# A Fourier-mixing layer in float32 pieces: product 2 of the first transform adds onto a copy of product 1 in an accumulator bank

## The chip, the core and the metric

The kernel runs on one core of a Trainium2 chip. The metric is the time of one execution on the device, in microseconds (us); each number of a run is one execution, and a version's time is the median of its runs. The engines are TensorE (PE in the profile; its weight loads are PEld), VectorE (DVE), ScalarE (ACT), GpSimd (POOL) and SyncE (SP, which here only issues transfers). Matmuls write accumulators into eight banks, each of 128 partitions by 512 float32; ScalarE and VectorE read them from there.

## The reference, cut to what matters

```python
def _A_ref(x, dft_seq_re, dft_seq_im, dft_hid_re, dft_hid_im):
    a = jnp.einsum("bsd,ed->bse", x, dft_hid_re)
    b = jnp.einsum("bsd,ed->bse", x, dft_hid_im)
    y = jnp.einsum("ts,bse->bte", dft_seq_re, a) - jnp.einsum("ts,bse->bte", dft_seq_im, b)
    return y

def _B_ref(x, w1, b1, w2, b2):
    y = _layernorm(x, axis=-1)
    h = _gelu(jnp.einsum("bsd,df->bsf", y, w1) + b1)
    return jnp.einsum("bsf,fd->bsd", h, w2) + b2

x = A_x
xn = _layernorm(x, axis=-1)
s = _A_ref(xn, A_dft_seq_re, A_dft_seq_im, A_dft_hid_re, A_dft_hid_im)
g = _silu(_B_ref(xn, B_w1, B_b1, B_w2, B_b2))
return x + s * g
```

There are 2048 tokens of 512 values, and the hidden layer of `_B_ref` has 1792. The *first transform* is the pair `a`, `b`: along the hidden dimension, with one 512 by 512 matrix for each.

## The kernel before, in words

All matrices are float32. For the matmuls each is split into a high part, rounded by ScalarE (`activation` with Copy into the matmul's input type), and the rest, which VectorE subtracts out; a product is then three matmuls (high by high, high by rest, rest by high).

The stages follow each other on TensorE: the first transform (with the statistics of the layer norm), the first layer of the network (`hy`, `hz`, `hx`), the second layer (`ma`, `mb`), and the second transform along the tokens (`px`, `pz`, `pw`), whose accumulators are multiplied by the gate and written out.

The tokens lie in 16 tiles of 128. Tiles 0 to 5 go through the first transform directly: 12 matmuls into one bank for `a`, 12 for `b` (`dft_mm`, L400; accumulators `pd`), evicted by ScalarE with the token's scale (`dft_out`, L425). Tiles 6 to 15 go in pairs through a scheme that gives the four blocks of a 2 by 2 block product by seven products instead of eight. One pair is done first (tau "u", tiles 6 and 7: accumulators `quy`, `quz`, `qux`), then four pairs (tau 1, chunk c = 0 to 3, tiles 8 + c and 12 + c: `q1y`, `q1z`, `q1x`). Product p has six matmuls per chunk (`q_mm`, L645), and `KEY_Q` says which of three accumulators it uses:

- y: product 1 starts it, then 6, 7 and 4 add to it
- z: product 5 starts it, 3 adds to it
- x: product 2 alone

After products 1, 5, 6 and 4 ScalarE evicts the accumulator, scaled per token, into a tile `e` in the on-chip memory (`q_after`, L631, the instruction at L637). After 2, 3 and 7 VectorE multiplies the accumulator by the scale and adds it to such a tile (L642), which is then a finished block: tile i's part of `a` is product 1 plus product 2. A finished block is appended to a list of stores, which SP issues in order, four behind (`q_out`, L626).

The order of work is written out by hand: each engine executes its instructions in the order of the program text. For the u pair the order of products is 1, 5, 6, 2, 7, 3, 4, with VectorE's work on 2 and 3 put later (`u_after`, L757 to L772). For the four pairs (L777 on) the order is 1, 2, 5, 3, 6, 7, 4, each over the four chunks. Between chunks stand steps that prepare operands of later products: `y_scale` (L542) and `y_sum` (L577) on VectorE, `y_round` on ScalarE (the helper at L77), `y_rest` on VectorE (L81). In product 1 the sum t1, which product 5 needs, is formed by VectorE after chunk 1 and rounded by ScalarE after chunk 2, so ahead of the eviction of chunk 3. In product 2, `post(2, c)` is VectorE's work on chunk c.

Banks come from a pool of eight (`bank`): a new accumulator takes a bank that is free, the one longest free first, and its first writer waits until that bank's last reader is done. The bank of y is taken at product 1, that of x at product 2, that of z at product 5. Tiles `e` come in the same way from the pool `op` of 39 tiles in the on-chip memory. After product 4 the bank pool is closed, and the next layer takes the same eight banks as four accumulators of two banks.

Of the kernel before, what the change touches and what calls it, by code (L numbers as in the profile page):

```python
# [11 lines left out]
AF = mybir.ActivationFunctionType  # L12
ALU = mybir.AluOpType
# [7 lines left out]
def fnet_mixer_kernel(ctx: ExitStack, tc: tile.TileContext, x, xT, ct, wt, w1, w2, b1, b2, out):  # L21
    nc = tc.nc
# [28 lines left out]
    def guest(name):  # L51
        return op.tile([P, 2, W], F32, tag="op", name=name)

    def bank(name):
        return psum.tile([P, W], F32, tag="ps", name=name)
# [366 lines left out]
    def dft_at(i, m):  # L422
        return (b_d if m else a_d)[tok(i) // 2][tok(i) % 2]
# [14 lines left out]
    def store():  # L438
        dst, e = stores.pop(0)
        nc.sync.dma_start(out=dst, in_=e)  # L440
# [165 lines left out]
    qx, q_part = {}, {}  # L606
    Q_TILES = {1: lambda c: (2 * NC + c, 3 * NC + c), "u": lambda c: (NC + CONV + c, NC + CONV + PAIRS + c)}

    def q_scale(tau, t):
        if tau == 1:  # L610
            return qq[:, t - HB:t - HB + 1], nq[:, t - HB:t - HB + 1]
        return rr[:, t:t + 1], nr1[:, t:t + 1]

    def q_at(tau, name, c):
        if tau == "u" and PAIRS == 1:
            return (tau, name in (1, 5)), int(name in (5, 4))
        return (tau, name, c // 2), c % 2

    def q_place(tau, name, c):
        key, at = q_at(tau, name, c)  # L620
        if key not in q_part:
            q_part[key] = guest(f"q{tau}{name}_{c}")
        return q_part[key][:, at, :]


    def q_out(i, m, e):  # L626
        stores.append((dft_at(i, m), e))
        while len(stores) > LAG:
            store()

    def q_after(p, c, tau=1):  # L631
        i, j = Q_TILES[tau](c)
        (f, nf), (g, ng) = q_scale(tau, i), q_scale(tau, j)
        acc = qx[tau, KEY_Q[p], c]
        if p in (1, 5, 6, 4):
            e = q_place(tau, p, c)
            nc.scalar.activation(e, acc, AF.Copy, scale={1: f, 5: ng, 6: g, 4: nf}[p])  # L637
            if p == 4:
                q_out(i, 1, e)
        else:  # L640
            e = q_place(tau, {2: 1, 3: 6, 7: 5}[p], c)
            nc.vector.scalar_tensor_tensor(e, acc, {2: f, 3: g, 7: ng}[p], e, op0=ALU.mult, op1=ALU.add)  # L642
            q_out(*{2: (i, 0), 3: (j, 0), 7: (j, 1)}[p], e)

    def q_mm(p, c, tau=1):  # L645
        key = tau, KEY_Q[p], c
        yh, yl = y_op[RIGHT[p], tau]
        if p in (1, 5, 2):
            qx[key] = bank(f"q{tau}{KEY_Q[p]}{c}")
        cols = slice(c * P, (c + 1) * P)  # L650
        terms = [(a[:, k, cols], w) for k in range(2)
                 for a, w in ((yh, a_op[p][k][0]), (yh, a_op[p][k][1]), (yl, a_op[p][k][0]))]
        for n, (a, w) in enumerate(terms):
            nc.tensor.matmul(qx[key], a, w, start=p in (1, 5, 2) and n == 0,  # L654
                             stop=p in (2, 3, 4) and n == len(terms) - 1, skip_group_check=True)

    def q_product(p, *steps):
        for c in range(NC):
            q_mm(p, c)
            if p in (1, 5, 6, 4):  # L660
                q_after(p, c)
            for do in steps[c:c + 1]:
                for o in do:
                    o()

    def u_product(p):
        for c in range(PAIRS):
            q_mm(p, c, "u")
            if p in (1, 5, 6, 4):
                q_after(p, c, "u")  # L670

    def u_after(p):
        for c in range(PAIRS):
            q_after(p, c, "u")
# [522 lines left out]
    for u, (p, j) in enumerate(m_units):  # L1197
# [3 lines left out]
        if u == 1:  # L1201

            n = NJ - 1
# [5 lines left out]
        n = NJ - 1  # L1209
# [9 lines left out]
        q = m_order.index(p)  # L1219
# [56 lines left out]
    acc, part = {}, {}  # L1276
# [124 lines left out]
```

## Time and profile before

| what | value |
|---|---|
| median of 3 runs | 665.37 us (664.99 to 666.4) |
| the profiled execution, its own time | 665.02 us |
| its span, first to last instruction | 663.2 us |
| its granted TensorE clock | 1.0 |
| matmuls | 2914 |
| first matmul of the u pair, of product 1 on the four pairs, of the next layer | 40.19, 49.73, 87.81 us |

The page of the profile gives the busy time of each engine and its share of the span, then the span in 40 slices (the granted clock in tenths of full speed), and the chain of work that ended last. In the lists, `out<-in` are the program's names for tiles, and L with a number is the line in the code. In an engine's order of time a row gives the start, the length, the engine, the line, the operation, its operands, their size, and in brackets the idle time ahead of it and what ended that. In the grouped list a row ends with the count, the busy time, the mean of one in ns and the idle time ahead of the group.

### The profile page before, as it was taken

What the parts mean: (1) busy time and instruction counts of PE and PEld (TensorE: products, weight loads), DVE (VectorE), ACT (ScalarE), POOL (GpSimd) and SP (SyncE); (2) the same over time, 40 slices, a digit from 0 to 9 for tenths busy, and PEclk for the clock granted to TensorE, in tenths of its full rate; (3) what the DMA queues carried; (4) which work ended last, traced back from release to release, by engine and by line L of the source; (5) the groups of instructions that cost most, each with busy time, mean ns of one, the idle gap of its engine ahead of it and who ended that gap; (6) DMA issues with size and microseconds to landing.
All of it is one profiled execution on the core that took longest, in us unless ns stands there. A gap on an engine that the chain in (4) does not pass through costs nothing.

```text
span 663.2 us, 8219 instructions
## 1 busy us (share of the span) xinstructions
PE 658.2 (99%) x2914; PEld 542.6 (82%) x2914; DVE 543.5 (82%) x584; ACT 361.4 (54%) x420; POOL 50.7 (8%) x84
## 2 busy tenths in 40 slices
PE   9999999999999999999999999999999999999997
PEld 6888888888888888888888888888888888888886
DVE  7899978877776866888979998739877299998986
ACT  6775467544446754555455544456444455646540
POOL 0002000321121100000000000000000001210100
PEclk9999999999999999999999999999999999999999
DMA  9879430987989999798699996416544558996984
GB/s 320 289 266 276 154 140 1 360 314 250 358 302 351 417 411 370 264 385 305 255 386 409 387 326 225 153 51 200 184 156 129 127 137 258 305 257 239 319 251 138
DMA packets 71877, 172.81 MB, mean 261 GB/s; under 512 B 6896, under 2 KB 22812, under 8 KB 71836
## 3 DMA queue, kind: packets, MB, share of 16 engines
q1 hardware_dynamic: 59488, 132.27, 56.7%
q0 software_dynamic: 12032, 39.86, 18.9%
q8 instruction: 23, 0.38, 0.2%
q10 hardware_dynamic: 316, 0.16, 0.1%
q14 instruction: 18, 0.15, 0.1%
HBM read 121.91 MB, written 50.35 MB: 260 GB/s over the span
## 4 chain that ended last, share of the span: by engine, by line
PE 99%; DVE 0%; issue 0%
PE pz L1015 20%; PE px L1015 18%; PE hy L830 11%; PE ma L1015 11%; PE mb L1015 9%; PE hz L830 6%; PE pw L1015 5%; PE pd L406 3%; PE q1y L654 3%; PE hx L830 3%; PE pd L418 2%; PE px L1336 2%; PE pw L1336 2%; PE q1z L654 2%; PE quy L654 1%; PE q1x L654 1%
## 5 line engine op out<-in xcount | busy, mean ns | idle before, releaser
L1121 DVE TENSOR_TENSOR c<-c,c 128x1024 f32<-128x1024 f32 x32 | 39.2, 1224 | 3.4 <-DMA c<-ct 3.4
L81 DVE TENSOR_TENSOR w1l<-w1r,w1h 128x1792 fp32r<-128x1792 f32 x7 | 14.2, 2024 | 20.9 <-ACT w1h L525 20.9
L835 ACT ACTIVATE hc<-hc,b_t 128x1024 f32<-128x1024 f32 (+1 forms) x18 | 17.3, 960 | 25.0 <-DVE hc L875 22.6
L63 DVE TENSOR_TENSOR R_b1l<-c,R_b1h 128x1024 fp32r<-128x1024 f32 x16 | 19.5, 1222 | 13.4 <-ACT R_b1h L62 10.1
L62 ACT ACTIVATE R_s3h<-c 128x1024 fp32r<-128x1024 f32 x16 | 17.0, 1062 | 23.8 <-DVE c L1121 9.8
L1015 PE MATMUL pw<-R_s1h,L 128*128 128x512 f32 x96 | 29.7, 389 | 0.0
L62 ACT ACTIVATE R_b2h<-c 128x1024 fp32r<-128x1024 f32 x16 | 16.9, 1058 | 21.9 <-DVE c L1126 15.5
L63 DVE TENSOR_TENSOR R_s2l<-c,R_s2h 128x1024 fp32r<-128x1024 f32 x16 | 19.6, 1224 | 8.6 <-PE pz L1015 8.6
L62 ACT ACTIVATE R_s2h<-c 128x1024 fp32r<-128x1024 f32 x16 | 17.0, 1060 | 16.8 <-PE px L1015 9.3
L63 DVE TENSOR_TENSOR R_s3l<-c,R_s3h 128x1024 fp32r<-128x1024 f32 x16 | 19.6, 1226 | 3.9 <-PE pz L1015 3.8
L62 ACT ACTIVATE R_s1h<-c 128x1024 fp32r<-128x1024 f32 x16 | 16.4, 1052 | 11.4 <-DVE c L1132 11.4
L1129 POOL DMA_DIRECT2D c<-ct x8 | 7.0, 872 | 200.9 <-DVE c L1126 162.9
L62 ACT ACTIVATE R_b1h<-c 128x1024 fp32r<-128x1024 f32 x16 | 16.6, 1051 | 9.4 <-PE px L1015 4.4
L62 ACT ACTIVATE R_a1h<-c 128x1024 fp32r<-128x1024 f32 x16 | 16.8, 1053 | 8.9 <-PE pz L1015 7.2
L1015 PEld LDWEIGHTS pw<-R_s1h,L 128*128 128x128 f32 x96 | 18.0, 188 | 3.7
L63 DVE TENSOR_TENSOR R_b2l<-c,R_b2h 128x1024 fp32r<-128x1024 f32 x16 | 19.4, 1220 | 1.5 <-PE px L1015 1.5
L63 DVE TENSOR_TENSOR R_a1l<-c,R_a1h 128x1024 fp32r<-128x1024 f32 x16 | 19.6, 1223 | 1.3 <-PE px L1015 1.1
L63 DVE TENSOR_TENSOR R_s4l<-c,R_s4h 128x1024 fp32r<-128x1024 f32 x16 | 19.6, 1226 | 0.7 <-PE px L1015 0.7
L1126 DVE TENSOR_TENSOR c<-c,c 128x1024 f32<-128x1024 f32 x16 | 19.6, 1224 | 0.4
L62 ACT ACTIVATE R_s4h<-c 128x1024 fp32r<-128x1024 f32 x16 | 16.8, 1049 | 5.2 <-PE pz L1015 5.0
L63 DVE TENSOR_TENSOR R_s1l<-c,R_s1h 128x1024 fp32r<-128x1024 f32 x16 | 18.9, 1221 | 0.4 <-ACT R_s1h L62 0.3
L62 ACT ACTIVATE w2h<-w 128x1024 fp32r<-128x1024 f32 (+1 forms) x14 | 13.2, 946 | 10.7 <-DVE w L943 3.9
(1003 smaller groups left out, 2227.3 us busy)
## 6 DMA issues: line engine op xcount, KB each, us to landing
c<-ct SPq DMA_DIRECT2D x68, 512.0 KB, 5.7
m<-h_d SPq DMA_DIRECT2D x48, 512.0 KB, 6.7
h_d<-ht POOLq DMA_DIRECT2D x21, 512.0 KB, 6.8
s_d<-sa SPq DMA_DIRECT2D x32, 256.0 KB, 4.0
la<-s_d SPq DMA_DIRECT2D x32, 256.0 KB, 6.7
h_d<-hc POOLq DMA_DIRECT2D x13, 512.0 KB, 3.8
x<-x SPq DMA_DIRECT2D x16, 256.0 KB, 5.4
sa<-a_d SPq DMA_DIRECT2D x8, 512.0 KB, 6.4
```

Of the source, the lines that this page charges most:

```text
L62: nc.scalar.activation(hi, src, AF.Copy)
L63: nc.vector.tensor_sub(lo, src, hi.bitcast(F32))
L81: nc.vector.tensor_sub(hi_lo[1], src, hi_lo[0].bitcast(F32))
L406: nc.tensor.matmul(acc, xt[i, k][px], weights[m * NK + k][pw], start=n == 0, stop=n == len(terms) - 1)
L418: nc.tensor.matmul(dacc[i, m], xt[i, k][px], weights[m * NK + k][pw], start=seen[i, m] == 0, stop=seen[i, m] == 3 * NK - 1)
L654: nc.tensor.matmul(qx[key], a, w, start=p in (1, 5, 2) and n == 0, stop=p in (2, 3, 4) and n == len(terms) - 1, skip_group_check=True)
L830: nc.tensor.matmul(acc[:, tau, :], w[:, W1_AT[p], k * P:(k + 1) * P], r[:, k, :], start=p in (1, 5, 2) and i == 0, stop=p in (2, 3, 4) and ...
L835: nc.scalar.activation(dst, src, AF.Gelu_apprx_tanh, bias=b1_t[:, row:row + 1])
L1015: nc.tensor.matmul(acc[k][:, tau, :], a, c[:, tau, :], start=first and i == 0, stop=last and i == len(terms) - 1, skip_group_check=True)
L1121: nc.vector.tensor_sub(t, t, raw)
L1126: nc.vector.tensor_add(raw, raw, t)
L1336: nc.tensor.matmul(acc[KEY[name]][k][:, tau, cols], a[k], c[:, tau, cols], start=False, stop=last and u == us[-1] and i == 2, skip_group_c ...
```

## The change

ScalarE copies product 1's accumulator, unscaled, into the bank of x, and product 2's matmuls add to it there, so that x holds product 1 plus product 2. ScalarE then evicts x once with the token's scale, and the block is finished. The bank of x is therefore taken at product 1, just ahead of that of y; the tile `e` of this block is taken at product 2. VectorE's multiply-add after product 2 is gone, in the u pair and in the four pairs. The calls of `q_after` stay where they are: for product 2 they are now ScalarE instructions at the places of `u_after(2)` and `post(2, c)`.

```diff
@@ in q_after
-        if p in (1, 5, 6, 4):
+        if p == 1:
+            nc.scalar.activation(qx[tau, "x", c], acc, AF.Copy)
+        elif p == 2:
+            e = q_place(tau, 1, c)
+            nc.scalar.activation(e, acc, AF.Copy, scale=f)
+            q_out(i, 0, e)
+        elif p in (5, 6, 4):
             e = q_place(tau, p, c)
-            nc.scalar.activation(e, acc, AF.Copy, scale={1: f, 5: ng, 6: g, 4: nf}[p])
+            nc.scalar.activation(e, acc, AF.Copy, scale={5: ng, 6: g, 4: nf}[p])
             if p == 4:
                 q_out(i, 1, e)
         else:
-            e = q_place(tau, {2: 1, 3: 6, 7: 5}[p], c)
-            nc.vector.scalar_tensor_tensor(e, acc, {2: f, 3: g, 7: ng}[p], e, op0=ALU.mult, op1=ALU.add)
-            q_out(*{2: (i, 0), 3: (j, 0), 7: (j, 1)}[p], e)
+            e = q_place(tau, {3: 6, 7: 5}[p], c)
+            nc.vector.scalar_tensor_tensor(e, acc, {3: g, 7: ng}[p], e, op0=ALU.mult, op1=ALU.add)
+            q_out(*{3: (j, 0), 7: (j, 1)}[p], e)
@@ in q_mm
-        if p in (1, 5, 2):
+        if p == 1:
+            qx[tau, "x", c] = bank(f"q{tau}x{c}")
+        if p in (1, 5):
             qx[key] = bank(f"q{tau}{KEY_Q[p]}{c}")
...
-            nc.tensor.matmul(qx[key], a, w, start=p in (1, 5, 2) and n == 0,
+            nc.tensor.matmul(qx[key], a, w, start=p in (1, 5) and n == 0,
                              stop=p in (2, 3, 4) and n == len(terms) - 1, skip_group_check=True)
```

## The prediction

> **What bounds the kernel now.** I read the page first (busy shares, granted clock, the chain that ended last), then the list of TensorE's waits, and after that the order of time of each engine from 40 to 90 us, where all the changed code runs.
>
> ```profile
> span 663.2 us, 8219 instructions
> ...
> PE 658.2 (99%) x2914; PEld 542.6 (82%) x2914; DVE 543.5 (82%) x584; ACT 361.4 (54%) x420; POOL 50.7 (8%) x84
> ...
> PEclk9999999999999999999999999999999999999999
> ...
> PE 99%; DVE 0%; issue 0%
> ```
>
> TensorE is busy for 658.2 of 663.2 us, its clock is never lowered, and the chain that ended last runs through it for 99%. A busy TensorE need not be a full one, since the matmuls of this trace overlap. So the second view is what TensorE waited for in the whole span:
>
> ```profile
> engine line waited for: us in total, times, longest us
> PE idle_ps L202 <- DVE warm L237: 1.2, 1, 1.2
> ```
>
> One wait of 1.2 us, ahead of the first instruction, and none after it. The third is TensorE's order of time at the change (start, length, matmul; six matmuls to a chunk of the block products, the first row of a chunk shown):
>
> ```profile
> 41.33 0.39 PE L654 MATMUL quy<-W,ul 128*128 128x512 f32 x1
> ...
> 44.27 0.62 PE L654 MATMUL qux<-W,uh 128*128 128x512 f32 x2
> ...
> 49.73 0.62 PE L654 MATMUL q1y<-W,y_1h 128*128 128x512 f32 x2
> ...
> 52.45 0.61 PE L654 MATMUL q1y<-W,y_1h 128*128 128x512 f32 x2
> ...
> 53.81 0.62 PE L654 MATMUL q1y<-W,y_1h 128*128 128x512 f32 x2
> ...
> 55.17 0.62 PE L654 MATMUL q1x<-W,y_1h 128*128 128x512 f32 x2
> ...
> 59.25 0.61 PE L654 MATMUL q1x<-W,y_1h 128*128 128x512 f32 x2
> ...
> 60.61 0.39 PE L654 MATMUL q1z<-A5h,yt_1h 128*128 128x512 f32 x1
> ...
> 64.69 0.39 PE L654 MATMUL q1z<-A5h,yt_1h 128*128 128x512 f32 x1
> ...
> 71.27 0.39 PE L654 MATMUL q1z<-A3h,y_1l 128*128 128x512 f32 x1
> ```
>
> From 60.61 to 71.27 there are 48 matmuls, so 47 steps of (71.27 - 60.61) / 47 = 0.227 us: each starts 0.227 us after the one before, though it lasts 0.39. A chunk is 6 x 0.227 = 1.36 us, and the chunks stand exactly that far apart (52.45 to 53.81 to 55.17). TensorE is issued full; 2914 matmuls at that pace are 661 us, the span. Only an edit that changes the number of matmuls, or makes TensorE wait, can move the end.
>
> **The change, part by part.** The number of matmuls stays: product 2 still has six per chunk. What differs for TensorE is that the first matmul of product 2 in each of the five chunks adds to its bank instead of starting it anew. The row at 71.27 is a matmul that adds (product 3 on product 5's bank), the row at 60.61 one that starts: 0.39 us each and the same step. Cost 0. No row shows a matmul that adds to what ScalarE wrote. Its bounds are nothing and five matmuls that lose their overlap, 5 x (0.39 - 0.227) = 0.8 us; I take nothing, because the nearest rows are those that add.
>
> VectorE loses five multiply-adds, the one below on qux and four on q1x:
>
> ```profile
> L642 DVE SCALAR_TENSOR_TENSOR q<-q1x,qq,q 128x512 f32<-128x512 f32 x4 | 2.9, 746 | 0.0
> ```
> ```profile
> 49.47 0.75 DVE L642 SCALAR_TENSOR_TENSOR qu<-qux,rr,qu 128x512 f32<-128x512 f32 x1
> 50.13 0.16 DVE L160 TENSOR_TENSOR qq<-vv,rr 128x8 f32<-128x8 f32 x1
> ...
> 50.61 1.22 DVE L542 TENSOR_TENSOR xT<-xT,rowR 128x1024 f32<-128x1024 f32 x1
> ...
> 52.88 0.75 DVE L642 SCALAR_TENSOR_TENSOR qu<-quz,rr,qu 128x512 f32<-128x512 f32 x1
> 53.54 1.22 DVE L81 TENSOR_TENSOR y_1l<-xT,y_1h 128x1024 fp32r<-128x1024 f32 x1
> 54.67 1.22 DVE L542 TENSOR_TENSOR xT<-xT,rowR 128x1024 f32<-128x1024 f32 x1
> 55.93 1.22 DVE L577 TENSOR_TENSOR xT<-xT,xT 128x1024 f32<-128x1024 f32 x1
> ...
> 62.45 0.75 DVE L642 SCALAR_TENSOR_TENSOR q<-q1x,qq,q 128x512 f32<-128x512 f32 x1
> ```
>
> Each is 0.75 us long and takes 0.66 us of VectorE's queue (49.47 to 50.13): 5 x 0.66 = 3.3 us. Nobody on the chain waits for that today, so it is worth 0 at the end; it only brings VectorE's later work forward. ScalarE, 54% busy, gets five evictions more. Its rows here:
>
> ```profile
> 41.75 0.69 ACT L637 ACTIVATE qu<-quy,rr 128x512 f32<-128x512 f32 x1
> ...
> 49.93 0.69 ACT L637 ACTIVATE qu<-quy,nr 128x512 f32<-128x512 f32 x1 [2.24 <-PE quy L654]
> 50.52 0.68 ACT L429 ACTIVATE e<-pd,nr 128x512 f32<-128x512 f32 x1
> 51.86 1.06 ACT L77 ACTIVATE y_1h<-xT 128x1024 fp32r<-128x1024 f32 x1 [0.66 <-DVE xT L542]
> 52.84 1.92 ACT L637 ACTIVATE q<-q1y,qq 128x512 f32<-128x512 f32 x3
> 57.25 1.06 ACT L77 ACTIVATE yt_1h<-xT 128x1024 fp32r<-128x1024 f32 x1 [2.49 <-DVE xT L577]
> 58.21 0.67 ACT L637 ACTIVATE q<-q1y,qq 128x512 f32<-128x512 f32 x1
> ```
> ```profile
> L846 ACT ACTIVATE hc<-hy 128x512 f32<-128x512 f32 x4 | 2.4, 588 | 0.7 <-PE hy L830 0.7
> ```
>
> No row has ScalarE writing an accumulator bank. The nearest are the same eviction into SBUF without a scale pointer, 0.59 us, and with one, 0.69; the far bound is 1.06, the time for twice the elements. I take 0.67, as the copy stands in the place of that row. The new eviction of product 2 has the form of the present one, 0.69, and takes 0.59 of the queue (49.93 to 50.52). Five of them are 2.9 us of ScalarE, beside TensorE's work.
>
> What matters is the new wait: TensorE may not start a chunk of product 2 before ScalarE has copied it. Behind that matmul stands all of TensorE's queue, so a late copy is paid in full. Five places:
>
> The u pair: product 1 ends at 41.33 + 0.39 = 41.72, the copy runs from 41.75 to 42.4, product 2 begins at 44.27. Spare 1.8 us. Its bank is wanted 44.27 - 41.75 = 2.5 us sooner, with three pd, quy and quz in use beside it, six of eight.
>
> The new eviction of qux stands on ScalarE behind the one at 50.52 and runs from 51.11 to 51.80; behind it waits the rounding at 51.86. That one waited for VectorE's L542 at 50.61, which now comes 0.66 earlier and ends at 51.17. So it starts at 51.70, not later than today, and so do chunks 0 to 2, copied by 54.7; the first is needed at 55.17, the others 1.36 us apart.
>
> The fourth chunk is the tight one. Its copy stands behind the rounding at 57.25, which waits for VectorE's subtraction at 55.93. VectorE has no gap between 49.47 and that row except 0.1 us ahead of it, so the removed 0.66 us reaches it: 55.27 to 56.49 (its predecessor, the row at 53.54, needs the rounding above, done at 51.70 + 1.06 = 52.76, and begins at 52.88). The rounding then runs from 56.59, the copy from 57.55 to 58.22; TensorE needs it at 59.25. Spare 1.0 us. With none of VectorE's gain and a copy of 1.06 us it ends at 58.21 + 1.06 = 59.27, and with 0.1 us from one engine to the next (57.15 to 57.25 above) TensorE waits 0.1 us.
>
> Banks: the second accumulator is now taken with the first, so all eight banks must be had by 53.81, where the eighth was first written at 59.25. The first four accumulators find banks that were emptied earlier, the last four take those of quy, pd, qux and quz as they come free: 50.62, 51.20, 51.80, and for quz 52.88 + 0.75 = 53.63, or 52.97 with the gain. TensorE itself writes only two of these, at 52.45 (from the second) and at 53.81 (from the fourth). Spare 1.2 and 0.8, or 0.2 without the gain.
>
> Product 2's evictions must be out before product 5 reuses the banks, from 60.61 on and the last at 64.69. On ScalarE they follow the copy from 58.2, three by 60.2, the fourth behind one more rounding by about 61.8; VectorE's last is done at 62.45 + 0.75 = 63.20 today. The stores on SP's queue keep their order. GpSimd's loads there read nothing that these steps write.
>
> Hand-over: the changed bank order also changes which of the next layer's accumulators inherits the one emptied last.
>
> ```profile
> 87.81 0.39 PE L830 MATMUL hy<-y_1h,w1h 128*128 128x512 f32 x1
> ```
> ```profile
> 88.01 0.69 ACT L637 ACTIVATE q<-q1y,nq 128x512 f32<-128x512 f32 x1 [0.67 <-PE q1y L654]
> ```
>
> The next layer starts at 87.81 without a wait, 0.9 us before the last eviction ends (88.70). So today its first accumulator has other banks. If it now got that one, TensorE would wait 88.70 + 0.1 - 87.81 = 1.0 us. Bounds 0 and 1.0; I take 0, since the two-bank accumulators of the next layer share out the eight banks as four pairs, and three of them are not the first one's.
>
> The sum is 0: five dropped multiply-adds hidden, five evictions hidden, every new wait met with at least 0.8 us to spare. Against the profiled execution's own 665.02 us (663.2 in the span, 1.8 around it) that is 665.0; the three runs have a median of 665.37, and on that scale I say 665.4. A measurement of this kernel can tell about 0.2%, 1.3 us, from no change.
>
> **Rivals.** Faster: TensorE is not as full as it looks, and VectorE paces it. For it: weight loads are busy for 82%, as VectorE is. The Trainium skill, Perfetto Trace Analysis, section Identifying the Most-Contended Engine, says that matmul busy time is no good measure of how near TensorE is to its limit, and to judge by weight-load busy time; by that rule 18% would be open here. Against it: the even step of 0.227 us and the missing waits. If it were so, the 3.3 us would come off: 661.7, on the medians' scale 662.1. Chance 3%.
>
> Slower: the banks decide. If the one of quz goes to an earlier chunk of product 1 than the last, TensorE waits there until 52.97 plus 0.1. For the third chunk (52.45) that is 0.6 us, still no change; from the second on (53.81 - 2 x 1.36 = 51.09) it is 2.0 us, so 667.0, on the medians' scale 667.4. For it: all eight are now in use at once and 5.4 us sooner. The Trainium skill, PSUM — Partial Sum Buffer, section Summary: rules for kernel authors, says to evacuate promptly because the space is tight; the change holds five banks one product longer. Against it: quz is the last to be freed, and banks go round in the order in which they come free. Chance 6%.
>
> Slower too: several of the small bounds at once (0.1 for the fourth copy, 0.8 for the adding matmuls, 1.0 for the hand-over): 1.9 us, 666.9, or 667.3 by the median. Each is against the nearest row, and any one alone stays within 0.2%. Chance 4%.
>
> That the change doesn't do what it says (product 2 overwrites instead of adding) would give the forecast's time, as the two kinds of matmul cost the same.
>
> **How the numbers follow.** 87% for the forecast, single small bounds included, 3% faster, 6 + 4 = 10% slower. The range starts 0.8 us under the lowest run, 664.2, and takes in most of the small bounds and the beginning of the bank case, up to 667.0; the faster rival and the upper end of the slower ones are left out.
>
> **What would show it.** In the changed profile: TensorE's list of waits still has the one row; product 2's chunks still start 1.36 us apart; the fourth copy ends near 58.2 and lasts 0.6 to 0.7 us; the subtraction at 55.93 comes 0.66 us earlier; VectorE is down by 5 x 0.75 = 3.7 us, ScalarE up by about 3. A wait of TensorE at q1y would speak for the banks, one at q1x for the copy, one at the first hy for the hand-over. The prediction is wrong if the median leaves 664.0 to 666.7.

## The result, and the profile after

The changed kernel takes 666.45 us (median of 14 runs, 666.11 to 668.43) against 665.28 us for the kernel before (14 runs, 664.99 to 666.4). The ratio is 1.002, with an interval of 1.0013 to 1.0027: a loss of 1.2 us, small but real. It lies 1 us above the forecast of 665.4, and inside both ranges that the prediction gives: 664.2 to 667.0 where its numbers are worked out, and 664.0 to 666.7 in its last line, whose upper end is 0.25 us away. The profiled execution took 666.13 us.

The page of the changed kernel, first the lines that answer to those of before:

```profile
span 664.3 us, 8216 instructions
...
PE 658.2 (99%) x2914; PEld 542.2 (82%) x2914; DVE 540.7 (81%) x579; ACT 364.8 (55%) x425; POOL 50.8 (8%) x84
...
PEclk9999999999999999999999999999999999999999
```

Nothing in these lines tells of a loss but the span: TensorE has the same busy time and the same number of matmuls, VectorE has five instructions and 2.8 us less, ScalarE five and 3.4 us more. What changed is in TensorE's list of waits:

```profile
engine line waited for: us in total, times, longest us
PE idle_ps L202 <- DVE warm L237: 1.2, 1, 1.2
PE hy L838 <- ACT q L643: 0.8, 1, 0.8
PE pt L321 <- DVE xc L295: 0.4, 1, 0.4
```

The last row stands at 4.8 us, ahead of all changed code; TensorE is 0.03 us behind the kernel before at 18 us, so it costs nothing that counts. The second row is new, and it is the sign that the prediction had named for the hand-over: the first matmul of the next layer waits for ScalarE at L643, an eviction. In TensorE's order of time (start, length, matmul, idle time ahead of it):

```profile
87.60 0.39 PE L662 MATMUL q1y<-W,yt_1l 128*128 128x512 f32 x1
88.77 0.50 PE L838 MATMUL hy<-y_1h,w1h 128*128 128x512 f32 x1 [0.78 <-ACT q L643]
89.11 0.40 PE L838 MATMUL hy<-y_1l,w1h 128*128 128x512 f32 x1
89.35 0.40 PE L838 MATMUL hy<-y_1h,w1l 128*128 128x512 f32 x1
...
90.28 0.39 PE L838 MATMUL hz<-yt_1h,w1h 128*128 128x512 f32 x1
```

and on ScalarE:

```profile
86.73 0.69 ACT L643 ACTIVATE q<-q1y,nq 128x512 f32<-128x512 f32 x1 [0.73 <-PE q1y L662]
88.03 0.69 ACT L643 ACTIVATE q<-q1y,nq 128x512 f32<-128x512 f32 x1 [0.61 <-PE q1y L662]
90.48 0.60 ACT L854 ACTIVATE hc<-hy 128x512 f32<-128x512 f32 x1 [1.76 <-PE hy L838]
```

The last eviction of product 4 ends at 88.03 + 0.69 = 88.72, and the first hy starts at 88.77. The step from 87.60 is 1.17 us where 0.23 is the pace, so 0.94 us is lost. The six matmuls from there on take 1.51 us (88.77 to 90.28) where six take 1.36, which is 0.15 more. Together 1.09 us, of the 1.17 us between the medians and the 1.1 us between the spans.

Next, what the prediction had worked out row by row at the change itself. ScalarE and VectorE of the changed kernel:

```profile
41.75 0.58 ACT L636 ACTIVATE qux<-quy 128x512 f32<-128x512 f32 x1
...
51.11 0.69 ACT L639 ACTIVATE qu<-qux,rr 128x512 f32<-128x512 f32 x1
51.68 1.07 ACT L77 ACTIVATE y_1h<-xT 128x1024 fp32r<-128x1024 f32 x1
...
56.46 1.06 ACT L77 ACTIVATE yt_1h<-xT 128x1024 fp32r<-128x1024 f32 x1 [1.79 <-DVE xT L577]
57.43 0.58 ACT L636 ACTIVATE q1x<-q1y 128x512 f32<-128x512 f32 x1
```
```profile
55.20 1.22 DVE L577 TENSOR_TENSOR xT<-xT,xT 128x1024 f32<-128x1024 f32 x1
```

The fourth copy ends at 58.01, and TensorE's fourth chunk starts on the pace:

```profile
59.27 0.62 PE L662 MATMUL q1x<-W,y_1h 128*128 128x512 f32 x2
```

### The profile page after: what moved, and what is told of

It reads as the page before. It is cut to its first block, busy times and chain, and to the rows that moved or that the text cites. A ratio compares the mean times of both kernels' runs of the same rounds, so it can differ in the third digit from the quotient of the medians.

```text
span 664.3 us, 8216 instructions
## 1 busy us (share of the span) xinstructions
PE 658.2 (99%) x2914; PEld 542.2 (82%) x2914; DVE 540.7 (81%) x579; ACT 364.8 (55%) x425; POOL 50.8 (8%) x84
## 4 chain that ended last, share of the span: by engine, by line
PE 99%; DMA 0%; DVE 0%; ACT 0%; issue 0%; DVEq 0%
PE pz L1023 20%; PE px L1023 18%; PE hy L838 12%; PE ma L1023 11%; PE mb L1023 9%; PE hz L838 6%; PE pw L1023 5%; PE pd L406 3%; PE q1y L662 3%; PE hx L838 3%; PE pd L418 2%; PE px L1344 2%; PE pw L1344 2%; PE q1z L662 2%; PE quy L662 1%; PE q1x L662 1%
```

## The experiments

**The theories.** *Hand-over:* the change gives q1y3, the accumulator that product 4 empties last, a bank of the pair that the next layer's first accumulator inherits, so TensorE waits at the seam of two stages (where one ends and the next begins), 30 us behind the last copy. *Rival:* the copies, the added evictions or the adding matmuls themselves cost the time. No view of the profile names the banks; this table is read out of the two programs as they were built:

```
               q1y0 q1y1 q1y2 q1y3   emptied last   the pair it is in, and who inherits that
before           6    5    1    7     q1y3 in 7      6 and 7: hz, which starts 1.36 us after hy
changed          6    1    3    0     q1y3 in 0      0 and 1: hy, the first
```

Each ratio below is against the kernel before in the same batch of runs: its median was 665.19 us beside the first, third, fourth and fifth experiment, and 665.3 us beside the others.

**The changed kernel, another order of chunks in product 4.** Only the order in which product 4 takes its accumulators differs: q1y2, in bank 3, now comes last, and q1y3 first.

```diff
-        for c in range(NC):
+        for n, c in enumerate((3, 1, 0, 2) if p == 4 else range(NC)):
...
-            for do in steps[c:c + 1]:
+            for do in steps[n:n + 1]:
```

> The changed kernel with one more edit: product 4 of the four pairs takes its chunks in the order 3, 1, 0, 2, so that the accumulator evicted last is q1y2 and not q1y3. Hand-over theory (the next layer's first accumulator inherits the bank of q1y3, which the change evicts last, and TensorE waits for that eviction): the wait at the first hy is gone, TensorE's list of waits is back to its one row, and the time is that of the kernel before, 665.3 us, ratio 1.000. Rival (the copies and the added evictions on ScalarE cost the time, wherever they stand): as the changed kernel, 666.4 us, ratio 1.002.

Measured: 666.47 us (11 runs), ratio 1.0018, 1.0009 to 1.0027. As slow as the changed kernel; by the time alone the rival has it. TensorE's waits say otherwise:

```profile
PE idle_ps L202 <- DVE warm L237: 1.2, 1, 1.2
PE q1y L662 <- DVE q L648: 0.8, 1, 0.8
PE pd L418 <- ACT xt L62: 0.5, 1, 0.5
```

The wait at hy is gone, and another of the same size stands at q1y, for VectorE at L648. In the order of time of VectorE, then of TensorE:

```profile
82.94 0.75 DVE L648 SCALAR_TENSOR_TENSOR q<-q1y,nq,q 128x512 f32<-128x512 f32 x1 [0.61 <-PE q1y L662]
```
```profile
82.51 0.39 PE L662 MATMUL q1y<-A7h,yt_1l 128*128 128x512 f32 x1
83.74 0.74 PE L662 MATMUL q1y<-W,yt_1h 128*128 128x512 f32 x2 [0.84 <-DVE q L648]
```

Product 7 still ended with q1y3, and product 4 now began with it: the matmul had to wait until VectorE had read product 7 out of that bank. The experiment made a wait of its own. The expectation missed that; the edit tells neither theory from the other by its time.

**The same with the order 0, 3, 1, 2.** q1y2 is again the last, and q1y3 the second.

```diff
+        for n, c in enumerate((0, 3, 1, 2) if p == 4 else range(NC)):
```

> The changed kernel, product 4 of the four pairs in the order 0, 3, 1, 2: q1y3 is no longer evicted last, and its chunk stands one chunk (1.36 us) behind product 7's last one, so that VectorE's eviction of product 7 from the same bank (0.8 us of waiting in the order 3, 1, 0, 2) fits ahead of it. Hand-over theory: no wait of TensorE, 665.3 us, ratio 1.000. Rival (the loss is the copies' and evictions', and only changes its place when the order changes): 666.4 us, ratio 1.002, with a wait elsewhere.

Measured: 665.27 us (11 runs), ratio 0.9998, 0.9989 to 1.0007. TensorE's waits:

```profile
engine line waited for: us in total, times, longest us
PE idle_ps L202 <- DVE warm L237: 1.2, 1, 1.2
```

All copies, evictions and adding matmuls are in this kernel, and the loss is gone. The hand-over theory asked for just that, and no cost that the rival could name is left.

**The kernel before, with the wrong chunk last.** Nothing of the change is in it; the order 0, 1, 3, 2 leaves q1y2, in bank 1, for the end.

```diff
+        for n, c in enumerate((0, 1, 3, 2) if p == 4 else range(NC)):
```

> The kernel before, without any of the change, but product 4 of the four pairs takes its chunks in the order 0, 1, 3, 2. In the kernel before the pair of banks of the first hy holds q1y2, which is here evicted last. Hand-over theory: TensorE waits about 0.8 us at the first hy, its next matmul starts about 0.95 us late, and the time rises by 1.0 to 1.2 us to 666.4, ratio 1.0015 to 1.002. Rival (ScalarE's copies): no copy, so no change, 665.3 us.

Measured: 666.53 us (11 runs), ratio 1.0019, 1.001 to 1.0028. The same row as in the changed kernel, by the line numbers of before:

```profile
PE hy L830 <- ACT q L637: 0.8, 1, 0.8
```

So the whole loss can be had without a copy.

**Half of the change: the u pair alone.**

```diff
-        if p in (1, 5, 6, 4):
+        new = tau == "u"
+        if p == 1 and new:
+            nc.scalar.activation(qx[tau, "x", c], acc, AF.Copy)
+        elif p == 2 and new:
...
+        elif p in (1, 5, 6, 4):
```

(This is against the kernel before. The other branches keep its form, and the banks and flags in `q_mm` are split in the same way.)

> The change for the u pair alone; the four pairs are as before. Hand-over theory: q1y0 to q1y3 then take the same banks as in the kernel before, so no wait, 665.3 us, ratio 1.000. Rival (each copy and eviction costs its share): one fifth of the loss, 0.2 us.

Measured: 665.01 us (11 runs), ratio 0.9999, 0.999 to 1.0008.

**The other half: the four pairs alone** (`new = tau == 1`).

> The change for the four pairs alone; the u pair is as before. Hand-over theory: the bank that q1y3 gets is then the one that pd5_1 leaves, which belongs to a later accumulator of the next layer, so no wait at the first hy, 665.3 us, ratio 1.000: each half of the change is free and only both together cost 1.2 us. Rival (each copy and eviction costs its share): four fifths of the loss, 0.9 us, 666.2 us, ratio 1.0014.

Measured: 665.28 us (11 runs), ratio 1.0, 0.9991 to 1.0009. In both halves TensorE's list of waits has the one row of before. Each half costs nothing, and the two together 1.2 us. A cost that belongs to each copy would add up; a place in the order in which the banks go round doesn't. In the programs as built, with the u pair as before, q1y3 gets bank 2; with the four pairs as before, it stays in 7.

**The whole change, one line moved.** VectorE's eviction of quz is written ahead of ScalarE's of qux, so quz's bank comes free first.

```diff
     dft_out(5, 1)
     y_rest("11", 1)
+    u_after(3)
     u_after(2)
...
     y_centre(3, 0)
-    u_after(3)
     y_rest("21", 1)
```

> The changed kernel with one line moved: VectorE's work on product 3 of the u pair stands ahead of ScalarE's on product 2, so the bank of quz comes free ahead of that of qux. Product 4 is as it was. Every copy, every added matmul and every eviction stays. Hand-over theory: q1y3 takes another bank than the first hy does, so no wait, 665.3 us, ratio 1.000. Rival (copies and evictions): as the changed kernel, 666.4 us.

Measured: 665.36 us (11 runs), ratio 1.0002, 0.9993 to 1.0011, again with the one wait of before. q1y3 has bank 2 here. This and the order 0, 3, 1, 2 are two ways to make the change harmless; neither beats the kernel before.

**Is the eviction what TensorE waits for, one for one?** Three idle copies stand ahead of it in the changed kernel: they copy the tile `idle` onto itself and touch no data of the computation.

```diff
+            if (tau, p, c) == (1, 4, 3):
+                for _ in range(3):
+                    nc.scalar.activation(idle, idle, AF.Copy)
             nc.scalar.activation(e, acc, AF.Copy, scale={5: ng, 6: g, 4: nf}[p])
```

> The changed kernel with three idle copies on ScalarE ahead of the last eviction of product 4, some 0.65 us each. ScalarE stood idle for 0.6 us ahead of that eviction, so it comes 2.0 - 0.6 = 1.4 us later. Hand-over theory: the wait at the first hy grows one for one, from 0.8 to about 2.2 us, and the time goes from 666.4 to 667.8, ratio 1.004. Rival (that eviction is not what TensorE waits for): as the changed kernel, 666.4 us.

Measured: 667.7 us (4 runs), ratio 1.0039, 1.0026 to 1.0053. ScalarE, then TensorE, in the profiled execution:

```profile
87.39 1.94 ACT L645 ACTIVATE idle<-idle 128x512 bf16<-128x512 bf16 x3
89.24 0.67 ACT L646 ACTIVATE q<-q1y,nq 128x512 f32<-128x512 f32 x1
```
```profile
87.68 0.39 PE L665 MATMUL q1y<-W,yt_1l 128*128 128x512 f32 x1
89.96 0.50 PE L841 MATMUL hy<-y_1h,w1h 128*128 128x512 f32 x1 [1.90 <-ACT q L646]
...
91.05 0.63 PE L841 MATMUL hy<-y_1h,w1h 128*128 128x512 f32 x1
```

The eviction ends at 89.91 and hy follows 0.05 us later, as in the changed kernel (88.72, then 88.77). Both come 1.19 us later than there, and the time is 667.7 - 666.45 = 1.25 us longer: one for one, within 0.1 us. The delay itself is smaller than expected (1.2 us and not 1.4), and the wait with it: it grew from 0.78 to 1.90 us, not to 2.2. The profiled execution is the slowest of the four; the last section says what else it shows.

**Is the new wait at the copy a real one?** The kernel of the order 0, 3, 1, 2, with four idle copies ahead of the copy of q1y3.

```diff
         if p == 1:
+            if tau == 1 and c == 3:
+                for _ in range(4):
+                    nc.scalar.activation(idle, idle, AF.Copy)
             nc.scalar.activation(qx[tau, "x", c], acc, AF.Copy)
```

> The kernel of the order 0, 3, 1, 2 with four idle copies of 128x512 on ScalarE ahead of the copy of q1y3, some 0.65 us each, 2.6 us in all. They touch no data of the computation. If the copy's wait is as the prediction has it (the copy ended at 58.0 in the changed kernel, TensorE's fourth chunk of product 2 began at 59.27, spare 1.26 us), TensorE waits 2.6 - 1.26 = 1.3 us at q1x, and the time rises by 1.3 to 1.6 us. If the copy is not what admits the chunk, nothing changes, 665.3 us.

Measured: 666.76 us (10 runs), ratio 1.0022, 1.0013 to 1.0031: 1.5 us more than the same kernel without the idle copies.

```profile
57.78 2.60 ACT L638 ACTIVATE idle<-idle 128x512 bf16<-128x512 bf16 x4
60.29 0.58 ACT L639 ACTIVATE q1x<-q1y 128x512 f32<-128x512 f32 x1
```
```profile
59.39 0.39 PE L665 MATMUL q1x<-W,y_1l 128*128 128x512 f32 x1
60.92 0.72 PE L665 MATMUL q1x<-W,y_1h 128*128 128x512 f32 x2 [1.14 <-ACT q1x L639]
```

The same copy and the same matmul in the kernel of the order 0, 3, 1, 2:

```profile
57.79 0.58 ACT L636 ACTIVATE q1x<-q1y 128x512 f32<-128x512 f32 x1
```
```profile
59.64 0.62 PE L662 MATMUL q1x<-W,y_1h 128*128 128x512 f32 x2
```

The step on TensorE is 60.92 - 59.39 = 1.53 us, 1.30 over the pace. The copy ends at 60.87 where it ended at 57.79 + 0.58 = 58.37 without the idle copies, 2.5 us later; its spare there was 59.64 - 58.37 = 1.27, and in the changed kernel 59.27 - 58.01 = 1.26. 2.50 - 1.27 is 1.23, and the matmul starts 0.05 us behind the copy's end: 1.28. The wait that the change adds is there, and it is hidden by that spare.

## Why the prediction was right, and where it failed

*The end goes by TensorE alone, and the number of matmuls stays.* Right. With the one wait taken out in two ways the time is 665.3 and 665.4 us, though VectorE has five instructions less and ScalarE five more. The rival in which VectorE paces TensorE, at 662.1 us, falls with that. (2914 matmuls at the pace are 661 us, 2 us short of the span that the text takes them for; no step hangs on it.)

*Adding to what ScalarE wrote costs nothing, bound 0.8 us.* Right: the two harmless versions hold all five such matmuls and take the time of before.

*The copies.* Right: no copy is waited for; three sizes were a little off. A copy into a bank takes 0.58 us, not 0.67: less than the same eviction with a scale pointer, and as long as the one without, the nearer row. The subtraction came at 55.20, not 55.27, and the fourth copy ended at 58.01, not 58.22; the spare was 1.26 us, not 1.0, and the run with the late copy shows that a longer delay is paid.

*VectorE down by 3.7 us.* It is down by 2.8: a row of 0.75 us overlaps with the one behind it (49.47 + 0.75 - 50.13 = 0.09 us) and as much with the one ahead (48.34 + 1.22 - 49.47), and busy time counts a stretch once, so 0.57 us goes with each, 5 x 0.57 = 2.8. It changes nothing at the end.

*Banks inside the first transform.* No wait, as forecast. (The prediction's remark that five banks are held one product longer is true of the four pairs; in the u pair, with the order 1, 5, 6, 2, it is three products.) But the order of the banks was wrong, and that is the step that failed. The text gave the last four accumulators the banks of quy, pd, qux and quz in the order of x2, y2, x3, y3, because the code asks for x ahead of y. In the built program y comes ahead of x each time: y2 has quy's bank, x2 pd's, y3 qux's, x3 quz's. That fits a rule by which the accumulator written first comes first, as TensorE writes y before ScalarE copies it to x. By the text's order q1y3 would have had quz's bank, number 4, which lies outside hy's pair of 0 and 1; it had qux's, number 0.

*The hand-over, "Bounds 0 and 1.0; I take 0".* The bound was right for the wait, which takes 0.94 us; the 0.15 us that the matmuls after it lose are in no term of the sum. The value 0 was not right: it was settled by odds (three of the four pairs are not the first one's), where the order of the banks could have been followed to its end, with y ahead of x. The row of before had said how near it was, with hy starting 0.9 us ahead of the end of the last eviction. A bound that a reordering alone can reach should have had a chance of its own; here it lay inside the 87% for the forecast, since 1.0 us stays under the 0.2%, 1.3 us, that the text had taken for the least that can be told from no change. The measured 1.17 us stays under it too, by 0.16 us, though 14 runs of each did tell it from nothing. So the range held by luck in part: the term that the sum had at 0 came in whole, and it happened to be smaller than the range was wide.

## What to carry to other kernels

Where one engine is full from end to end, an edit's price isn't its work on the others but the one wait it may bring. Look for that wait also where the next stage begins and buffers change hands. Follow the order in which buffers go round, by first writes and last reads, up to that place, rather than going by the odds. And when a repair leaves the time as it was, read the waits before dropping the theory: here the repair had made a second wait of the same 0.8 us.

## What the runs showed of the hardware

In the profiled execution of the late eviction, a wait of 1.90 us was followed by matmuls at half pace (91.05 to 91.48 and on, 0.43 us apart where 0.227 is the pace). The table by stage (the second column is the stretch, then busy times of PE, PEld, DVE, ACT and POOL, the granted clock, the share of DMA and GB/s) shows it:

```profile
85.00:89.96 4.96, 3.07 (x14) 2.21 (x12) 3.37 (x3) 3.73 (x6) 0.00 (x0) 1.00 0.42 159
89.96:93.60 3.64, 3.64 (x9) 2.83 (x10) 0.00 (x0) 1.03 (x2) 0.00 (x0) 0.56 0.19 72
93.60:97.00 3.40, 3.40 (x16) 2.82 (x15) 2.21 (x2) 3.38 (x5) 0.00 (x0) 0.97 0.00 0
```

The granted clock was 1.00 up to the end of the wait and 0.56 in the mean of the 3.6 us behind it, and that execution took 668.85 us with a mean clock of 0.997, where the other three took 667.5 to 667.8 with 1.0. The Trainium skill, TensorE: Matmul & The Clock Gate, section Why this matters for your kernels, says to have no idle gaps over some 3 us between bursts of matmuls, as an idle window of TensorE brings the clock to one half. The row has a clock near one half behind a wait, but a wait of 1.90 us, shorter than the page's, and in one execution of four; no run varies the wait to show that it was the cause. The waits of 0.78 to 1.14 us in the other profiled executions left the clock at 1.0; in the changed kernel the six matmuls from the end of such a wait took 0.15 us more than six take.
